# The opening of an attention and MLP kernel: q of the first unit turned by VectorE, filler products on TensorE, and other shapes of the first loads

## The chip, the cores and the metric

The kernel runs on one core of a Trainium2 chip. The metric is the device time of one execution in microseconds (us); lower is better. The median of three runs before the change is 677.4 us.

## The reference

Two blocks follow one another. The first is a gated linear attention with an outer-product state, over 4 batches x 8 heads, 768 tokens, head size 48:

```python
f = 1.0 / (1.0 + np.exp(-f_logit))
for t in range(S):
    state = f[:, :, t, :, None] * state + np.einsum('bhd,bhe->bhde', k[:, :, t], v[:, :, t])
    y[:, :, t] = np.einsum('bhd,bhde->bhe', q[:, :, t], state)
```

Its result, 3072 rows of 8 x 48 = 384 values, is the input x of the second block:

```python
h = x @ w_in                              # 384 -> 2048
g = h * (1.0 / (1.0 + np.exp(-1.702 * h)))
out = g @ w_out                           # 2048 -> 384
```

q, k, v, f_logit and the output are float32. The two weight matrices come in float64, and the kernel itself makes float32 of their bits.

## The kernel before, in words

The tokens are worked on in 12 units of 256 tokens, three to a batch, all heads of a unit at once. Feature and head lie on the partitions: two heads of a pair on partitions 0 to 47 and 64 to 111, and four pairs by 256 tokens along the free dimension (1,024 columns). The inputs come from memory with tokens on the partitions, so each of f, q and k of a unit has to be turned. Tile `raw` holds the three inputs as loaded (index j: 0 is f, 1 is q, 2 is k). `F` holds the turned gates after the sigmoid and `X` the turned k and q.

There are two ways to load and turn. For units below `N_FILL` = 3, `load_raw` (L243) loads by pair of heads, four transfers of 32 partitions each, and `turn` (L324) multiplies slices of `raw` by the identity on TensorE (L338) and lets ScalarE copy the result out of PSUM (L341). For later units `load_raw` loads two shifted copies of each head's rows (L257, `lo` = 0 and 32), and VectorE turns 32x32 blocks in one instruction (L326).

The attention of a unit goes through six levels (blocks of 1, 2, 4, ... 32 tokens). At each level TensorE makes scores of keys and queries (`score`, L383), VectorE multiplies keys and queries by the gates of the level (`promote`, L435 and L436 in the first three units, L438 later), masks the scores (`evacuate`, L409), and ScalarE sets keys aside (`set_aside`, L422). TensorE then multiplies the masked scores with v (L447). GpSimd makes the products of gates for all levels ahead of time (`begin_gates`, L375). In the first two units v is put in order by products with a permutation (`load_vl`, L283), copied out by ScalarE (L287). The result `yT` (L570) goes by transfer into `xT`, the input of the MLP.

The weights come in pairs of pieces (`fetch_weights`, L166, transfers at L179 into a tile `bits`). `begin_pair` has ScalarE scale the high words (L207, tile `a`), and a chain of five VectorE instructions for each piece (L222, L218, L225, L226, L227) makes float32 of them. `convert` sends one instruction of that chain, and the plan places these calls between the parts of attention.

The order of work on each engine is the order in which it is written; `merge` (L734) mixes parts of attention of unit n with MLP work of earlier units (L619 for the first product, L645 for the second) by shares of columns. All loads are issued by SyncE, in order. The opening (L769 to L784) issues the loads of unit 0 in the order f, q, k, then a first pair of weights, then v; turns f, q, k; sends four steps of conversion; fetches two more pairs of weights; and loads unit 1. Unit 0 has no MLP work to be mixed with.

```python
    for fn in units[0][0]:
        fn()
    for _ in range(4):
        convert()
```

`units[0][0]` is `(begin_f, begin, begin_k, begin_gates)`: turn f, turn q (with the edge copies on GpSimd at L356 and L357), turn k, products of gates.

Of the kernel before, what the change touches and what calls it, by code (L numbers as in the profile page):

```python
# [9 lines left out]
F32 = mybir.dt.float32  # L10
# [13 lines left out]
def kernel(  # L24
# [32 lines left out]
    nc = tc.nc  # L57
    B, H, S, D = q.shape
    DM = H * D
    DFF = moe_w_in.shape[1]  # L60
    P = 128
    C = 64
    G = 128
    U = 256
# [3 lines left out]
    NP = H // 2  # L68
# [7 lines left out]
    N_FILL = 3  # L76
# [10 lines left out]
    ps = ctx.enter_context(tc.tile_pool(name="ps", bufs=1, space=bass.MemoryType.PSUM))  # L87
# [9 lines left out]
    R = U // 32  # L97
    RW = R * D + HS - D
    raw = const.tile([P, 3, NP, R * D], F32, name="raw")
    by_pair = [raw.rearrange("p j a x -> p j (a x)")[:, j, :2 * RW].rearrange("p (h x) -> p h x", h=2) for j in range(3)]  # L100
    for j in range(3):
        nc.gpsimd.memset(by_pair[j][:, :, R * D:], 0.0)

    ident = const.tile([P, P], F32, name="ident")
# [2 lines left out]

    masks = const.tile([P, NL, 64], F32, name="masks")
    at = [wp.tile([P, 64], I32, tag="bits", name=f"at{j}", bufs=PAIRS_AHEAD) for j in range(2)]
    for a in (2, 3):  # L110
        nc.gpsimd.memset(raw[:, :, a, R * D - 32:], 0.0)
    nc.gpsimd.iota(at[0], pattern=[[0, 64]], base=0, channel_multiplier=1)
    nc.gpsimd.iota(at[1], pattern=[[1, 64]], base=0, channel_multiplier=0)
    nc.vector.tensor_scalar(at[0], at[0], 63, None, op0=ALU.bitwise_and)
# [125 lines left out]
            fetch_weights()  # L240


    def load_raw(n, j, engine=nc.sync):  # L243
        if n >= NALL:
            return
        b, s0 = n // NU, n % NU * U
        src = (f_logit, q, k)[j]
        if n < N_FILL:
            for a in range(NP):
                engine.dma_start(  # L250
                    out=by_pair[j][32 * a:32 * (a + 1), :, :R * D],
                    in_=src[b, 2 * a:2 * a + 2, s0:s0 + U, :].rearrange("h (i j) d -> i h (j d)", j=R),
                )
            return
        for r in range(4):
            lo = 32 * (r % 2)
            engine.dma_start(  # L257
                out=raw[32 * r:32 * (r + 1), j, :, :R * D - lo],
                in_=src[b, r // 2::2, s0:s0 + U, :].rearrange("a (i j) d -> i a (j d)", j=R)[:, :, lo:],
            )  # L260
# [30 lines left out]
    def load_vn(n):  # L291
        if n >= NALL:
            return
        vns[n] = (mlp if n == 1 else ld).tile([P, NG, DM], F32, tag="osb" if n == 1 else "vn", name=f"vn_{n}", bufs=1)
        if n < N_TURN:
            b, s0 = n // NU, n % NU * U
            for g in range(NG):
                nc.sync.dma_start(
                    out=vns[n][:, g].rearrange("p (h d) -> p h d", h=H),
                    in_=v[b, :, s0 + g * P:s0 + (g + 1) * P, :].rearrange("h p d -> p h d"),  # L300
                )
            return
        nc.sync.dma_start(out=vns[n], in_=v_toks[n % 2].rearrange("(g p) e -> p g e", g=NG))
# [8 lines left out]
    def attention(n):  # L312
# [9 lines left out]
            return lambda fn: parts.append((kind, fn))  # L322

        def turn(j, out, fn=None):  # L324
            if n >= N_FILL:
                nc.vector.transpose(  # L326
                    out.rearrange("p (a i j) -> p a j i", a=NP, j=R),
                    raw[:, j].rearrange("p a (j d) -> p (a j) d", j=R)[:, :, :32],
                )
                if fn:  # L330
                    nc.scalar.activation(out, out, fn)  # L331
                return
            for j0 in range(0, R, 4):
                pt = ps.tile([P, 4, P], F32, tag="mm", name=f"t_{n}_{j}_{j0}", bufs=4)
                for jj in range(4):
                    for h in range(2):
                        x = (j0 + jj) * D
                        nc.tensor.matmul(  # L338
                            pt[h * HS:(h + 1) * HS, jj, :], lhsT=by_pair[j][:, h, x:x + HS], rhs=ident, start=True, stop=True
                        )  # L340
                nc.scalar.activation(  # L341
                    out.rearrange("p (a i j) -> p a i j", a=NP, j=R)[:, :, :, j0:j0 + 4],
                    pt.rearrange("p j (a i) -> p a i j", a=NP), fn or AF.Copy,
                )

        def begin_f():
            turn(0, F, AF.Sigmoid)
            if n:
                load_raw(n + 1, 0)

        def begin():
            turn(1, X[:, J, 1:])


            q_last[n] = att.tile([P, NP], F32, tag="q_last", name=f"q_last_{n}", bufs=2)
            nc.gpsimd.tensor_copy(q_last[n], view(X, J * NX + U, [[U, NP]]))  # L356
            nc.gpsimd.tensor_copy(view(X, J * NX, [[U, NP]]), q_last[n - 1])  # L357
            if n:
                load_raw(n + 1, 1)

        def begin_k():
            turn(2, X[:, 1, :NA])
            if n:
                load_raw(n + 1, 2)
            if n >= N_FILL:
                set_aside(0, True)
                promote(0)
# [333 lines left out]
    units = [attention(n) for n in range(NALL)]  # L701
# [68 lines left out]
        load_raw(0, j)  # L770
    fetch_weights()
    load_vn(0)
    for fn in units[0][0]:
        fn()
    for _ in range(4):
        convert()
# [49 lines left out]
```

## Time and profile before

| | |
|---|---|
| three runs | 676.33, 677.4, 679.3 us |
| span of the profiled execution | 674.0 us |
| TensorE busy | 652.6 us (97%) |
| VectorE busy | 378.4 us (56%) |
| ScalarE busy | 226.4 us (34%) |
| first scores (L383) start | 12.46 us |
| first MLP product (L619) starts | 50.95 us |
| read from memory | 56.92 MB |

Engines: PE is TensorE, PEld its load of weights, DVE VectorE, ACT ScalarE, POOL GpSimd, SP SyncE, which issues the loads. A product in float32 leaves two MATMUL records. Times in the timeline count from the start of the span. In the slices each digit is the busy share of a 40th of the span in tenths. PEclk is the granted clock of TensorE. In the chain of waits each line is a start, a length and what the chain consisted of at that time. In the timeline, brackets give the idle time ahead of an instruction and what ended it. A transfer has an issue, which is what the SP rows show, and lands some time later.

### The profile page before, as it was taken

What the parts mean: (1) busy time and instruction counts of PE and PEld (TensorE: products, weight loads), DVE (VectorE), ACT (ScalarE), POOL (GpSimd) and SP (SyncE); (2) the same over time, 40 slices, a digit from 0 to 9 for tenths busy, and PEclk for the clock granted to TensorE, in tenths of its full rate; (3) what the DMA queues carried; (4) which work ended last, traced back from release to release, by engine and by line L of the source; (5) the groups of instructions that cost most, each with busy time, mean ns of one, the idle gap of its engine ahead of it and who ended that gap; (6) DMA issues with size and microseconds to landing.
All of it is one profiled execution on the core that took longest, in us unless ns stands there. A gap on an engine that the chain in (4) does not pass through costs nothing.

```text
span 674.0 us, 19354 instructions
## 1 busy us (share of the span) xinstructions
PE 652.6 (97%) x8514; PEld 486.5 (72%) x8514; DVE 378.4 (56%) x675; ACT 226.4 (34%) x459; POOL 50.3 (7%) x116
## 2 busy tenths in 40 slices
PE   5879999999999999999999999999999999999997
PEld 4656766757777886886886886876886786786774
DVE  3999877887666546545546546445446444430440
ACT  4564443343134233333333233233233233231210
POOL 3020020010002002002002002002002001000000
PEclk9789999999999999999999999999999999999999
DMA  8877973571063535415415415415414103001000
GB/s 193 226 192 193 240 160 89 152 185 37 24 159 107 154 66 149 109 38 148 115 33 152 110 37 148 113 37 144 115 37 115 37 24 84 15 1 36 13 1 24
DMA packets 67551, 67.62 MB, mean 100 GB/s; under 512 B 30410, under 2 KB 61290, under 8 KB 67466
## 3 DMA queue, kind: packets, MB, share of 16 engines
q1 hardware_dynamic: 67466, 66.38, 38.6%
q8 instruction: 67, 1.10, 0.7%
q14 instruction: 18, 0.15, 0.1%
HBM read 56.92 MB, written 8.65 MB: 97 GB/s over the span
## 4 chain that ended last, share of the span: by engine, by line
PE 89%; DVE 7%; ACT 2%; issue 1%; DMA 1%; SPq 0%; DVEq 0%; ACTq 0%
PE h L619 37%; PE o L645 35%; PE sc L383 5%; PE y L447 5%; PE t L338 2%; PE y L562 2%; PE tkn L504 1%; PE sc L522 1%; DVE s L218 1%; DVE A L409 1%; DMA xT<-yT 1%; PE tv L283 1%; ACT yT L570 1%; DVE X L436 1%; DVE X L438 1%
## 5 line engine op out<-in xcount | busy, mean ns | idle before, releaser
L619 PE MATMUL h<-xT,w_in 128*128 128x256 f32 (+1 forms) x1152 | 261.1, 382 | 1.1 <-DVE sum L690 0.8
L645 PE MATMUL o<-w_out,g 128*128 128x384 f32 x768 | 259.6, 491 | 0.9 <-DVE g L625 0.9
L619 PEld LDWEIGHTS h<-xT,w_in 128*128 128x128 f32 x1152 | 215.8, 190 | 36.8 <-issue 3.5
L645 PEld LDWEIGHTS o<-w_out,g 128*128 128x128 f32 x768 | 143.0, 190 | 94.5 <-issue 2.2
L625 DVE TENSOR_TENSOR g<-h,sg 128x256 f32<-128x256 f32 (+1 forms) x192 | 80.8, 422 | 133.1 <-ACT sg L624 132.6
L624 ACT ACTIVATE sg<-h 128x256 f32<-128x256 f32 (+1 forms) x192 | 73.2, 383 | 169.4 <-PE h L619 164.1
L422 ACT COPY Kc<-X 128x512 f32<-128x512 f32 x69 | 45.9, 666 | 123.7 <-DVE X L438 87.3
L438 DVE TENSOR_TENSOR X<-X,tot 128x1024 f32<-128x1024 f32 x45 | 55.2, 1226 | 54.8 <-PE sc L383 50.1
L409 DVE TENSOR_TENSOR A<-sc,masks 128x512 f32<-128x512 f32 x72 | 46.7, 679 | 0.0
L326 DVE STREAM_TRANSPOSE X<-raw 128x1024 f32<-128x1024 f32 x18 | 36.7, 2039 | 16.7 <-PE y L562 13.9
L447 PE MATMUL y<-A,vl 64*48 64x64 f32 x2304 | 41.7, 219 | 0.0
L447 PEld LDWEIGHTS y<-A,vl 64*48 64x48 f32 x2304 | 36.8, 122 | 5.3 <-issue 5.0
L375 POOL TENSOR_TENSOR tot<-F 128x512 f32<-128x512 f32 x12 | 12.5, 1039 | 340.5 <-DVE st L539 327.9
L383 PE MATMUL sc<-X,Kc 48*64 48x64 f32 x1344 | 29.0, 224 | 6.8 <-ACT Kc L422 4.6
L383 PEld LDWEIGHTS sc<-X,Kc 48*64 48x64 f32 x1344 | 24.6, 138 | 13.8 <-ACT Kc L422 7.2
L570 ACT COPY yT<-y 48x512 f32<-48x512 f32 x48 | 27.8, 580 | 20.0 <-PE y L562 19.4
L331 ACT ACTIVATE F<-F 128x1024 f32<-128x1024 f32 x9 | 9.5, 1057 | 49.0 <-DVE F L326 49.0
L375 POOL TENSOR_TENSOR tot<-tot 128x256 f32<-128x256 f32 (+4 forms) x60 | 23.7, 395 | 4.7
L542 DVE TENSOR_TENSOR st<-st,sc 128x192 f32<-128x192 f32 x44 | 15.6, 354 | 15.1 <-PE sc L522 13.7
L338 PE MATMUL t<-ident,raw 128*64 128x128 f32 x288 | 19.6, 298 | 4.4 <-DMA raw<-in_f_logit_dram 4.4
L338 PEld LDWEIGHTS t<-ident,raw 128*64 128x64 f32 x288 | 18.4, 153 | 7.0 <-issue 6.1
L664 ACT COPY osb<-o 128x384 f32<-128x384 f32 x18 | 8.6, 478 | 41.5 <-PE o L645 41.5
(66 smaller groups left out, 385.0 us busy)
## 6 DMA issues: line engine op xcount, KB each, us to landing
vl<-v_tok SPq DMA_DIRECT2D x60, 192.0 KB, 2.8
bits<-in_moe_w_out_dram SPq DMA_DIRECT2D x8, 768.0 KB, 9.8
bits<-in_moe_w_in_dram SPq DMA_DIRECT2D x8, 576.0 KB, 7.9
v_tok<-in_v_dram SPq DMA_DIRECT2D x10, 384.0 KB, 4.3
vn<-v_tok SPq DMA_DIRECT2D x10, 384.0 KB, 6.0
xT<-yT SPq DMA_DIRECT2D x24, 144.0 KB, 2.7
raw<-in_f_logit_dram SPq DMA_DIRECT2D x18, 192.0 KB, 3.9
raw<-in_q_dram SPq DMA_DIRECT2D x18, 192.0 KB, 3.1
```

Source lines behind the costliest of these rows:

```text
L326: nc.vector.transpose(out.rearrange("p (a i j) -> p a j i", a=NP, j=R), raw[:, j].rearrange("p a (j d) -> p (a j) d", j=R)[:, :, :32],)
L338: nc.tensor.matmul(pt[h * HS:(h + 1) * HS, jj, :], lhsT=by_pair[j][:, h, x:x + HS], rhs=ident, start=True, stop=True)
L375: nc.gpsimd.tensor_tensor(tn, t2[:, :, 0], t2[:, :, 1], ALU.mult)
L383: nc.tensor.matmul(out[g * HS:(g + 1) * HS, h, a, :], lhsT=lhs(h, a * U + g * G), rhs=rhs(h, a * U + g * G), start=True, stop=True,)
L409: nc.vector.tensor_tensor(A[:, :, c:c + w].rearrange("p h (x t) -> p h x t", t=64), t["sc"][:, :, c:c + w].rearrange("p h (x t) -> p h x t ...
L422: nc.scalar.copy(c.rearrange("p (n m) -> p n m", m=m), X[:, j, :NA].rearrange("p (n two m) -> p n two m", two=2, m=m)[:, :, hf, :],)
L438: nc.vector.tensor_tensor(qk, qk, by, ALU.mult)
L447: nc.tensor.matmul(dst(h, g, a), lhsT=vls[n, u][g * 64:(g + 1) * 64, (2 * a + h) * D:(2 * a + h + 1) * D], rhs=A(h, g, a), start=(start an ...
L619: nc.tensor.matmul(ph, lhsT=w_in[:, c, ff * P:(ff + 1) * P], rhs=xTs[n][:, c, :], start=(c == 0), stop=(c == NK - 1))
L624: nc.scalar.activation(sg, ph, AF.Sigmoid, scale=1.702)
L625: nc.vector.tensor_tensor(g[ff // FG][:, ff % FG, :], ph, sg, ALU.mult)
L645: nc.tensor.matmul(t["po"], lhsT=g[ff // FG][:, ff % FG, tt * P:(tt + 1) * P], rhs=w_out[:, ff, :], start=(ff == ffs[0]), stop=(ff == ffs[ ...
```

## The change

It concerns the start, before there is MLP work to fill TensorE. q of unit 0 is loaded in the form of the later units and turned by VectorE, which has nothing to do there. While TensorE waits for the first load, it makes six products of the identity with itself, into a tile that nothing reads; the intent is to have its clock raised when the real work comes. Units 0 to 2 load by head of a pair: two transfers of 128 partitions each instead of four of 32. k of unit 0 comes in two halves by token (four transfers), so that the first half can be turned while the second is under way. The order of the opening becomes f, gates, q, k. The memsets of the padding of `raw` are moved to fit: GpSimd now clears the tail of q's part in the later form for all four pairs.

```diff
-    for j in range(3):
+    for j in (0, 2):
         nc.gpsimd.memset(by_pair[j][:, :, R * D:], 0.0)
@@
-    for a in (2, 3):
-        nc.gpsimd.memset(raw[:, :, a, R * D - 32:], 0.0)
+    for a in range(NP):
+        nc.gpsimd.memset(raw[:, :, a, R * D - 32:] if a > 1 else raw[:, 1, a, R * D - 32:], 0.0)
@@
+    def by_vector(n, j):
+
+        return n >= N_FILL or (n == 0 and j == 1)
+
     def load_raw(n, j, engine=nc.sync):
...
-        if n < N_FILL:
-            for a in range(NP):
-                engine.dma_start(
-                    out=by_pair[j][32 * a:32 * (a + 1), :, :R * D],
-                    in_=src[b, 2 * a:2 * a + 2, s0:s0 + U, :].rearrange("h (i j) d -> i h (j d)", j=R),
-                )
+        if not by_vector(n, j):
+            for x in ((slice(0, R // 2), slice(R // 2, R)) if n == 0 and j == 2 else (slice(0, R),)):
+                for h in range(2):
+                    engine.dma_start(
+                        out=by_pair[j][:, h, x.start * D:x.stop * D],
+                        in_=src[b, h::2, s0:s0 + U, :].rearrange("a (i j) d -> a i (j d)", j=R)[:, :, x.start * D:x.stop * D],
+                    )
             return
@@
         def turn(j, out, fn=None):
-            if n >= N_FILL:
+            if by_vector(n, j):
                 nc.vector.transpose(
@@
-    for fn in units[0][0]:
+
+    warm = ps.tile([P, P], F32, tag="mm", name="warm", bufs=4)
+    for _ in range(6):
+        nc.tensor.matmul(warm, lhsT=ident, rhs=ident, start=True, stop=True)
+    begin_f, begin, begin_k, begin_gates = units[0][0]
+    for fn in (begin_f, begin_gates, begin, begin_k):
         fn()
```

On VectorE the change adds one instruction, the transpose, ahead of the first conversion (L222); the order behind it stays. On ScalarE it takes away the two copies of q. On SyncE there are ten issues ahead of the first weights instead of twelve.

## The prediction

> **What bounds the kernel now.** I read the page's slices first, to see where TensorE is not full.
>
> ```profile
> PE 652.6 (97%) x8514; PEld 486.5 (72%) x8514; DVE 378.4 (56%) x675; ACT 226.4 (34%) x459; POOL 50.3 (7%) x116
> ...
> PE   5879999999999999999999999999999999999997
> ...
> DVE  3999877887666546545546546445446444430440
> ...
> PEclk9789999999999999999999999999999999999999
> DMA  8877973571063535415415415415414103001000
> ```
>
> A slice is 16.85 us. From the fourth on TensorE is full, so what an opening saves is kept to the end. Only in the first three slices is something else the bound, and there VectorE shows a 9 from the second slice on. Next the chain of waits, asked for the first 75 us.
>
> ```profile
> 4.40 7.22 PE t L338 x96
> ...
> 11.70 0.46 ACT X L341
> 12.16 0.12 issue
> 12.28 0.99 ACT a L207 x2
> ...
> 13.61 1.16 DVE s L218 x2
> 14.77 0.62 DVE X L435
> ...
> 43.12 0.04 issue
> 43.16 0.48 PE y L562 x11
> ...
> 47.49 1.13 PE sc L383 x32
> ```
>
> The opening's turns (96 records at L338) lead to the last copy of X, ScalarE goes on to `a` (L207, the first weight pair), and from 13.3 to 43.1 the chain is VectorE almost without a break. That is 30 of the 47 us before TensorE takes over. The time is therefore set by the moment at which VectorE gets going. The timeline says what it waits for.
>
> ```profile
> 12.28 0.98 ACT L207 ACTIVATE a<-bits 128x384 f32<-128x384 f32 x2
> ...
> 12.85 0.83 DVE L222 TENSOR_SCALAR a<-a 128x384 int32<-128x384 int32 x2 [9.57 <-ACT a L207]
> ...
> 14.69 0.70 DVE L435 TENSOR_TENSOR X<-X,F 128x512 f32<-128x512 f32 x1
> ```
>
> VectorE sat idle for 9.57 us, and what released it was a conversion of weights, not the scores. The first product of attention with a gate (L435) stands behind four conversion instructions. So the load of the first weight pair (`bits`, from L179) matters as much as q, f and k. The completion records of the trace give its two transfers 11.52 and 12.12 us, the four of f 2.75 to 4.26, of q 4.79 to 6.14, of k 6.57 to 8.10, and v 13.08 and 14.19. In the kernel before ScalarE came free (12.28) just after the weights had landed (12.12): two ends within 0.2 us, of which the change moves one. Last, the issues and the loads by stage:
>
> ```profile
> 0.74 1.80 SPq L250 DMA_DIRECT2D raw<-in_f_logit_dram  x4
> 2.58 1.84 SPq L250 DMA_DIRECT2D raw<-in_q_dram  x4
> 4.46 1.84 SPq L250 DMA_DIRECT2D raw<-in_k_dram  x4
> 6.35 0.93 SPq L179 DMA_DIRECT2D bits<-in_moe_w_in_dram  x2
> ```
> ```profile
> 0.00:5.00 5.00, 0.60 (x6) 0.63 (x8) 1.25 (x8) 1.28 (x1) 2.40 (x20) 1.00 0.47 134
> 5.00:10.00 5.00, 5.00 (x68) 5.00 (x66) 0.00 (x0) 1.95 (x4) 0.00 (x0) 1.00 0.85 220
> 10.00:15.00 5.00, 3.91 (x66) 2.33 (x62) 2.06 (x5) 2.96 (x5) 3.65 (x8) 1.00 1.21 213
> ```
>
> The last two columns are the DMA share and GB/s. An issue takes 0.46 us and brings 98 kB, so the raw loads are paced by their issue, at about 210 GB/s. From 10 us on the engines are over-full.
>
> **What the Trainium skill says.** "TensorE: Matmul & The Clock Gate", What's actually happening: the array runs at half clock until a window of about 3.4 us has been busy, and windows run freely. The trace agrees: the first 40 records at L338 took 3.7 us (4.4 to 8.1), the next 41 took 1.8, and the low spells later (21.7 to 28.5, 45.6 to 52.4) last two windows each. The same page, Architectural detail: ScalarE and VectorE are strict FIFO; the 9.57 us above, with L435 behind it, agree. "DMA: Bandwidth & Descriptors", Queues, rings and completion order: loads issued on one queue share a ring per engine and are consumed in order. The landings above are in order of issue. So bytes put ahead of the weights delay the weights.
>
> **The change part by part.**
>
> *f.* Two transfers of 197 kB are issued by 1.6 us. First bytes came at 1.8 before; 393 kB at 210 to 300 GB/s end at 3.1 to 3.7 us, against 4.26.
>
> *Products of the identity.* Six full 128x128 products. The chain has 4 records of L504 (two products of this size) at 0.44 us with the clock up, so 0.44 each at half clock, and six last 2.6 us: about 1.5 (the identity is ready) to 4.1. They end when f is there; f itself gains 0.3 us at most from its earlier landing. They move the end of the half-clock spell from 8.0 towards 5 us. The 32 records of f then take 1.4 us (at full clock) to 3.0 (half); ScalarE's F is done at 6.3 to 7.8 against 8.7.
>
> *q by VectorE.* This removes 32 records at L338 and two ScalarE copies of 0.72 us, and adds one transpose of 2.04 us (the row of L326). It lies in VectorE's 9.57 us of idling, so it costs nothing if q is there by about 9.5. The price is bytes: q comes in the form with two shifted copies, 4 heads x 384 or 352 floats on 32 partitions, 753 kB in place of 393. A load of this form later in the trace (k, issued at 299.7) completed 5.0 us after its first issue. Here the first issue waits for a GpSimd memset (some 1.85 us against 1.6), so q lands near 6.9 and is turned near 8.9.
>
> *k in halves.* Four transfers of 98 kB, issued 3.6 to 5.4, land behind q at 7.3 to 8.6. Each half takes 16 records (0.7 us) and a ScalarE copy (0.72). The last X is done at 8.8 to 10.1 against 12.16.
>
> *First scores.* They start at about 9 to 10.3 us instead of 12.46. Behind them TensorE waits for v. The gates' products on GpSimd, now issued ahead of the edge of q, take 3.7 us from about 7 and are needed only after 15.
>
> *Weights.* All raw loads are now 1,533 kB against 1,180. At 225 to 290 GB/s from 1.8 us they end at 7.1 to 8.6; I take 7.7 (before: first weight packets at 7.4). The first weight pair then took 4.7 us, with a slow first microsecond (158 GB/s from 7 to 8 against 240 and 283 in the next two). As SyncE issues it 0.9 us sooner than before (10 transfers ahead in place of 12), part of that should be hidden: 3.8 to 4.7, I take 4.2. The pair lands at 10.9 to 13.3, by my values at 11.9. ScalarE, idle by then, starts `a` at 11.95 instead of 12.28. So of the 2 to 3.4 us that the scores gain, 0.3 us reach VectorE; the rest becomes a wait of ScalarE for `bits`, with `L222` and behind it `L435` waiting for that.
>
> *Later units.* Units 1 and 2 load with 6 transfers each in place of 12. SyncE waits less, but VectorE, full from 13 to 43 us, hides this. The second weight pair landed at 18.9 and was wanted by VectorE at 20.7 with 1 us of ScalarE between, so a gain above some 0.8 us would need that load to come sooner too.
>
> Sum: 677.4 - 0.3 = 677.1 us.
>
> **The rivals.** *The scores' gain arrives:* the weights land by about 9.5 and the chain starts where X is ready. For it: the DMA engines were only 70 to 72% busy from 3 to 7 us. Against it: 786 kB of weights behind 1,533 kB need 2,319 kB in 7.7 us, 300 GB/s, above any 5 us stretch shown. Partly so, gain 1.5 to 3 us: 675.0. *The doubled q delays the weights:* landing at 13.3, 1.0 us late, the second pair also late, and TensorE cold when its scores of unit 0 come, since it now idles from 10 to 13 us; plus 1.0 to 1.5: 678.7. For it: share 1.21 from 10 to 15; against it: the issue pacing that goes away. *Only the clock:* a half-clock spell at 45.6 to 52.4 falls into TensorE's own stretch from 47.5 on and costs about half of 4.9 us. Where the free windows fall decides whether it is one window or two: 1.7 us either way, in both kernels. It widens every case and favours none.
>
> **How the numbers follow.** Weights bound, 677.1: 0.63. Gain arrives, 675.0: 0.22. Weights later, 678.7: 0.15. With about 1.5 us of spread from the clock (before: 676.33 to 679.3) the range 674.5 to 679.3 leaves out about two in ten. Half a per cent is 3.4 us: faster than 674.0 needs the best of the first rival and a lucky clock, 0.10; slower than 680.8 the worst of the second, 0.05; within, 0.85.
>
> **What would show it.** Right: ScalarE's first `a` waits for the load of `bits`, near 12 us; VectorE's L222 follows within 0.8 us; the scores at L383 begin near 10 us and gain nothing. Wrong: if L222 starts before 11 us, the weights were not the bound and the time falls by about as much; if after 13, the second rival holds. The transpose of q ending after 12 us would show q's load mis-sized. If L222 starts on time and yet the end moves by more than 2 us, the reason lies after 43 us, most likely in the clock.

## The result and the profile after

The changed kernel takes 694.69 us (median of 4 runs, 694.1 to 695.11) against 677.46: a ratio of 1.0251, 95% interval 1.0227 to 1.0275. It is 17.2 us slower, far outside the stated range of 674.5 to 679.3.

The slices of the page after, in the same rows as before:

```profile
PE 660.1 (95%) x8494; PEld 491.4 (71%) x8494; DVE 380.2 (55%) x676; ACT 225.1 (32%) x457; POOL 49.3 (7%) x117
...
PE   5775998999999999999999999999999999999998
...
DVE  1795887778676645545545545545546444431450
...
PEclk9687999999999999999999999999999999999999
DMA  5675697267016443523523524514503202101000
```

The loss lies in the first four slices (17.3 us each). TensorE's fourth slice is a 5 where it was a 9, and VectorE's first is a 1 where it was a 3. The DMA row is lower there than before, 5675 against 8877, although more bytes are to be moved. The stretch up to TensorE's first MLP product, before (to 50.95 us) and after (to 67.70), says how large it is:

```profile
0.00:50.95 50.95, 36.73 (x840) 27.69 (x841) 37.92 (x88) 25.97 (x45) 10.06 (x36) 0.88 0.83 203
0.00:67.70 67.70, 42.62 (x821) 31.76 (x821) 40.56 (x92) 24.75 (x44) 8.83 (x37) 0.81 0.65 162
```

The columns are the stretch, its length, the busy time of TensorE, of its weight loads, of VectorE, ScalarE and GpSimd, then the granted clock, the DMA share and GB/s. Of the 19.0 us by which the two spans differ, 16.8 are there when the MLP starts. TensorE is idle for 10.9 us more and busy for 5.9 us more at a lower mean clock (0.81 against 0.88). So the core waits for loads, while its DMA engines are less busy than before. The chain of waits for the first 75 us of the kernel after:

```profile
1.55 8.00 DMA raw<-in_f_logit_dram
...
9.57 8.69 DMA raw<-in_k_dram
...
18.30 2.41 PE t L343 x18
...
35.98 9.46 DMA bits<-in_moe_w_out_dram
...
48.04 12.19 DMA bits<-in_moe_w_in_dram
60.23 7.43 DMA xT<-yT
```

Before, this chain held 2.15 us of loads. Now five transfers hold 46 us of it. The timeline after shows what this does to the instructions that the prediction named (line numbers are 5 to 10 higher here):

```profile
1.47 2.93 PE L781 MATMUL warm<-ident 128*128 128x128 f32 x12 [1.47 <-POOL ident masks.py:199]
...
9.60 3.67 PE L343 MATMUL t<-ident,raw 128*64 128x128 f32 x30 [2.70 <-DMA raw<-in_f_logit_dram]
...
12.82 2.02 DVE L331 STREAM_TRANSPOSE X<-raw 128x1024 f32<-128x1024 f32 x1 [9.47 <-DMA raw<-in_q_dram]
...
21.94 0.82 DVE L222 TENSOR_SCALAR a<-a 128x384 int32<-128x384 int32 x2 [7.10 <-ACT a L207]
```

The last field names the wait: f is complete at 9.6 us instead of 4.26, q is turned from 12.8, and VectorE's chain, which the prediction put at about 12.5, starts at 21.94. The six products missed their purpose here: they ended at 4.40, and the 30 records of f that begin at 9.60 took 3.67 us, where e1 below needs 2.78 for 32. By stage, for the kernel after (last two columns: DMA share and GB/s):

```profile
0.00:5.00 5.00, 2.93 (x12) 2.63 (x12) 1.26 (x8) 1.28 (x1) 2.47 (x21) 1.00 0.25 73
5.00:10.00 5.00, 1.08 (x6) 0.69 (x8) 0.00 (x0) 0.00 (x0) 0.00 (x0) 1.00 0.73 139
10.00:15.00 5.00, 4.00 (x34) 3.20 (x30) 2.02 (x1) 1.19 (x2) 1.01 (x1) 1.00 0.50 133
```

Before, the same stretches moved at 134, 220 and 213 GB/s. The completion records say why. In the kernel before, each transfer of f leaves 16 marks within 0.5 us (the first: 2.43 to 2.75). In the kernel after, each of the two transfers of f has one mark shortly after its issue (1.87 and 2.53 us) and four later: 5.44 to 6.17, and 9.15 to 9.56. Each transfer of q, which is cut in the other form, has twelve marks early and four late: 5.50 to 6.54, then 9.80 to 10.50 for the first of them. Read with one mark for each engine that ends its share, four of the sixteen engines carry f and k, the other twelve have no share of them, and four are late with their share of what is issued behind.

There is a second effect, on SyncE. It sends the third transfer of k at 6.19 us, directly behind the last mark of f's first transfer (6.17), and the fourth at 9.57, behind that of f's second (9.56). The first weights wait behind k and the last mark of q's first transfer (10.50):

```profile
4.17 6.34 SPq L255 DMA_DIRECT2D raw<-in_k_dram  x4
10.55 2.58 SPq L179 DMA_DIRECT2D bits<-in_moe_w_in_dram  x2
```

They were issued at 6.35 before. So the twelve engines, done with q at 9.08, have nothing to do until the weights go out. This is not the main part: in e3 below the weights go out at 6.22, and their last mark is still at 19.84, against 20.81 here.

The Trainium skill states the rule for the number of engines in "DMA: Bandwidth & Descriptors", Why a DMA increments its semaphore by 16 and not by 1: the number of engines is the largest one up to 16 that divides the size of the slowest dimension of both access patterns, they are the lowest-numbered ones, and the issuing engine makes up the missing marks at once. (Which of the sixteen they are, the marks here do not tell.) In the changed `load_raw` the memory side is `a (i j) d -> a i (j d)`, with the head of a pair outermost, 4 of them; before it was `i h (j d)`, with 32 token groups outermost. The marks, one early and four late, agree with four engines.

### The profile page after: what moved, and what is told of

It is laid out like the page before. It is cut to its first block, busy times and chain, and to the rows that moved or that the text cites. A ratio compares the mean times of both kernels' runs of the same rounds, so it can differ in the third digit from the quotient of the medians.

```text
span 693.0 us, 19290 instructions
## 1 busy us (share of the span) xinstructions
PE 660.1 (95%) x8494; PEld 491.4 (71%) x8494; DVE 380.2 (55%) x676; ACT 225.1 (32%) x457; POOL 49.3 (7%) x117
## 4 chain that ended last, share of the span: by engine, by line
PE 85%; DMA 7%; DVE 4%; ACT 2%; issue 1%; SPq 0%; DVEq 0%; ACTq 0%
PE h L624 36%; PE o L650 34%; PE sc L388 5%; PE y L452 4%; DMA xT<-yT 2%; DMA bits<-in_moe_w_in_dram 2%; PE y L567 1%; DMA bits<-in_moe_w_out_dram 1%; PE tkn L509 1%; PE sc L527 1%; DMA raw<-in_k_dram 1%; PE t L343 1%; DMA raw<-in_f_logit_dram 1%; DVE X L443 1%; DVE A L414 1%
## 5 line engine op out<-in xcount | busy, mean ns | idle before, releaser
L331 DVE STREAM_TRANSPOSE X<-raw 128x1024 f32<-128x1024 f32 x19 | 38.7, 2038 | 26.1 <-PE y L567 13.9
L380 POOL TENSOR_TENSOR tot<-F 128x512 f32<-128x512 f32 x12 | 12.5, 1039 | 348.9 <-DVE st L544 325.4
L343 PEld LDWEIGHTS t<-ident,raw 128*64 128x64 f32 x256 | 17.5, 157 | 11.8 <-DMA raw<-in_f_logit_dram 5.2
L547 DVE TENSOR_TENSOR st<-st,sc 128x192 f32<-128x192 f32 x44 | 15.6, 354 | 15.1 <-PE sc L527 13.7
```

What stands on the lines that cost most here:

```text
L331: nc.vector.transpose(out.rearrange("p (a i j) -> p a j i", a=NP, j=R), raw[:, j].rearrange("p a (j d) -> p (a j) d", j=R)[:, :, :32],)
L343: nc.tensor.matmul(pt[h * HS:(h + 1) * HS, jj, :], lhsT=by_pair[j][:, h, x:x + HS], rhs=ident, start=True, stop=True)
L380: nc.gpsimd.tensor_tensor(tn, t2[:, :, 0], t2[:, :, 1], ALU.mult)
```

## The experiments

Theory E: the outermost index of 4 puts the loads on four engines, and that is the whole loss. Rivals: transfers to 128 partitions, or fewer and larger ones, are slow in themselves; the doubled q delays the weights; TensorE's idle time and its clock make the loss.

**e1: all of the change, with the token group outermost.** The partitions are then in the order token group, head, so ScalarE reads the turned tile in that order.

```diff
-in_=src[b, h::2, s0:s0 + U, :].rearrange("a (i j) d -> a i (j d)", j=R)[...]
+in_=src[b, h::2, s0:s0 + U, :].rearrange("a (i j) d -> i a (j d)", j=R)[...]
-pt.rearrange("p j (a i) -> p a i j", a=NP)
+pt.rearrange("p j (i a) -> p a i j", a=NP)
```

> All of the change is kept, but in the transfers of f, k (and q of units 1 and 2) the index of the token group (32) stands ahead of the index of the head (4) in the memory pattern, so partitions are in the order token group, head; bytes, packets, count of transfers and the 128 partitions are those of the changed kernel. Theory E (four engines): a transfer whose outermost index counts 4 runs on 4 of the 16 DMA engines; with 32 outermost it runs on 16. Then f lands by 4 us instead of 9.6, the first scores start before 12 us, and the time is 675 to 679 us. Rival S (transfers to 128 partitions, or fewer transfers in flight, are slow): still 690 us or more. Rival Q (the 753 kB of q ahead of the weights are the delay): still 690 us or more.

Measured: 679.53 us, ratio to before 1.0006 (0.9993 to 1.0019). f is complete at 4.35, the first scores start at 11.71. Bytes, shapes and counts of transfers are those of the changed kernel, so rivals S and Q fall: the order of two indices (with the order in which ScalarE reads, which follows from it) is worth 2.4%. TensorE's busy time falls back with it, from 660.1 to 653.2 us (652.6 before), so the lower clock of the kernel after was a consequence of the waits. Against the kernel before, all of the change together then comes to nothing that is measured here. The later runs show that this is two effects of opposite sign.

**e2, e3, e4: the kernel before with nothing but the loads by head,** for units 0 to 2, for unit 0, and for units 1 and 2.

```diff
-for a in range(NP):
-    engine.dma_start(out=by_pair[j][32 * a:32 * (a + 1), :, :R * D],
-        in_=src[b, 2 * a:2 * a + 2, s0:s0 + U, :].rearrange("h (i j) d -> i h (j d)", j=R))
+for h in range(2):
+    engine.dma_start(out=by_pair[j][:, h, :R * D],
+        in_=src[b, h::2, s0:s0 + U, :].rearrange("a (i j) d -> a i (j d)", j=R))
```

> The kernel before, with nothing of the change but the loads by head of a pair for f, q and k of units 0 to 2 (two transfers of 128 partitions, head index of 4 outermost). Theory E: this alone makes the loss, 690 to 700 us; since q too is now on four engines in unit 0, rather more than the changed kernel. Rival Q (the doubled q) and a rival in which the idle TensorE and its clock make the loss: 676 to 680 us.

> The kernel before, with the loads by head for unit 0 alone. Theory E: the start of VectorE's chain moves by the later landing of k and the weights, as in the changed kernel (22.4 against 13.3 us): 9 to 13 us more, 686 to 690 us. If units 1 and 2 make most of the loss: under 680 us.

> The kernel before, with the loads by head for units 1 and 2 alone. Theory E: the waits for weights and for the first MLP input between 36 and 68 us (9.5, 12.2 and 7.4 us in the chain of the changed kernel), less what other work hides: 5 to 9 us more, 682 to 687 us; e3 and e4 together give about the loss of e2. If unit 0 makes the whole loss: under 679 us.

Measured: e2 694.96 us, ratio 1.0232 (1.0207 to 1.0257), the loss of the changed kernel without filler products and without VectorE's transpose. e3 684.57, ratio 1.0085 (1.0061 to 1.011). e4 687.22, ratio 1.0119 (1.0098 to 1.014). The parts, 5.8 and 8.1 us (0.0085 and 0.0119 of 678.99), make 13.9 of e2's 15.8. e4 came out at the upper edge of what I expected. e3 missed: VectorE's L222 moved by the expected 9.2 us (22.02 against 12.85) and TensorE's first MLP product by 8.8 (59.73 against 50.95), but the median by only 5.8. The two traces do not settle this. That of e3 is of its slowest execution (686.28 us, median 684.57), that of the kernel before is of one (675.73 us) faster than all 23 that ran beside e3 (677.25 to 681.65, median 678.99). This makes 5.0 of the 10.5 us between the two traced executions; where the slower executions of the kernel before lose their time is in no trace. In e4 the loads of unit 0 are those of before. From its chain of waits:

```profile
32.45 8.66 DMA bits<-in_moe_w_in_dram
...
52.94 7.45 DMA xT<-yT
```

The weights and the first MLP input, neither of which the change touched, wait for the four engines behind the loads of units 1 and 2. The marks show it: the first transfer of `xT`, issued at 50.94, has twelve marks from 53.10 to 53.62 and four from 58.91 to 59.80. TensorE's first MLP product (its line here is L626) shows what it costs:

```profile
60.48 4.24 PE L626 MATMUL h<-xT,w_in 128*128 128x256 f32 x10 [6.28 <-DMA xT<-yT]
```

It starts 9.5 us later than before (50.95), and 6.28 us of idling ahead of it end with `xT`.

**e11: two heads in each transfer,** unit 0 alone, everything else as before.

```diff
+for a in (0, 2):
+    for h in range(2):
+        engine.dma_start(out=by_pair[j][32 * a:32 * a + 64, h, :R * D],
+            in_=src[b, 2 * a + h:2 * a + h + 3:2, s0:s0 + U, :].rearrange("a (i j) d -> a i (j d)", j=R))
```

> As e3 (unit 0 by head, units 1 and 2 as before), but each transfer takes two of the four heads: 64 partitions, outermost index 2, twice as many transfers of half the size. Theory E: two engines carry f, q and k instead of four; in e3 1,180 kB took 15.6 us on four (19 GB/s each), so about 31 us here, k lands near 33 us and the time is 14 to 18 us over e3 (697 to 703 us). Rival (it is the shape of 128 partitions, or few large transfers, that is slow): no slower than e3, 676 to 686 us.

Measured: 698.73 us, ratio 1.0296 (1.0275 to 1.0318), 14.2 us over e3 by the medians. The transfers of f, q and k have two late marks each, and the last of k comes at 29.82 us (17.43 in e3, 8.10 before). By stage, for e11:

```profile
10.00:15.00 5.00, 3.62 (x32) 3.27 (x30) 0.00 (x0) 0.60 (x1) 0.00 (x0) 1.00 0.13 50
15.00:20.00 5.00, 1.04 (x8) 0.52 (x8) 0.00 (x0) 0.60 (x1) 0.00 (x0) 0.95 0.13 49
```

A DMA share of 0.13 is two sixteenths: two engines fully busy, at 25 GB/s each, and fourteen idle. Halving the outermost index halves the engines, with smaller transfers to fewer partitions. The rival of shape could not give this.

**e14: as e2, with the token group outermost** (the two lines of e1's diff are all that differs from e2).

> The kernel before with loads in two transfers of 128 partitions for units 0 to 2, as e2, but with the token group (32) outermost in the memory pattern instead of the head (4): e2 and this differ in the order of two indices and in the pattern with which ScalarE reads the turned tile. Theory E: about 677 us against 694.96 of e2, ratio to before 0.997 to 0.999 as in e12. Rival (two transfers of 128 partitions are bad whatever the order): over 690 us. If ratio is 1.000 or more, the gain of e12 came from k in halves or the changed order of the opening.

Measured: 676.91 us, ratio to before 0.9976 (0.9964 to 0.9987). Against e2's 694.96 this is the plainest pair: one order of two indices, with ScalarE's reading to match. The same stretches in e14:

```profile
0.00:5.00 5.00, 0.85 (x4) 0.48 (x6) 1.25 (x8) 1.28 (x1) 2.40 (x20) 1.00 0.51 149
5.00:10.00 5.00, 5.00 (x54) 5.00 (x54) 0.00 (x0) 1.30 (x3) 0.00 (x0) 1.00 0.98 244
```

It is also faster than the kernel before, by 0.24%. The cause of that gain is open. In the traces VectorE's L222 starts later than before (13.71 against 12.85) and yT is made no sooner (44.69 against 44.39), but the traced execution of the kernel before (675.73 us) is faster than all 25 beside e14 (from 675.9), and the traced one of e14 (677.62) is slower than its median, so these two traces cannot show a gain.

**What the rest of the change is worth** was tried on the repaired loads, because the prediction rested on it. e6 turns q of unit 0 on TensorE again (`by_vector` is `n >= N_FILL`, with the old memsets); e12 is e6 without the six products; e10 is the kernel before with the six products alone.

> As e1 (token group outermost, all else of the change), but q of unit 0 is loaded once (393 kB instead of 753) and turned by TensorE as before the change. My theory W (the first weights hold VectorE's chain, and the doubled q holds the weights): the weights land about 1 us sooner than in e1, VectorE's L222 starts at 12.6 to 13.0 us instead of 13.66, and the time is 0.5 to 1 us under e1 (ratio to before 0.998 to 0.9995). Rival (q's turn by VectorE is worth what the change wanted): slower than e1 by 1 us or more, since X is ready later.

> As e6 without the six products. If the loads in two transfers make e6's gain over before: 676.8 us, ratio 0.997 to 0.999, as e6. If the products (and where TensorE's clock then falls) make it: ratio 0.9995 to 1.001. X is ready at 12 us or later, close to the landing of the weights at 12.5.

> The kernel before with the six products of the identity alone. Theory W (the first weights hold VectorE's chain): the turns end about 1.5 us sooner (96 records in 5.7 us as in e6 instead of 7.2), X is ready near 10.6 us, and ScalarE then waits for the weights, which land at 12.1 as before; L222 at 12.7 against 12.85, ratio 0.9985 to 1.0005. Rival (the turns hold the chain): L222 near 11.3 us and 1.5 us less (ratio 0.998 or lower).

Measured: e6 676.76, ratio 0.998 (0.9971 to 0.999); e12 677.32, ratio 0.9975 (0.9963 to 0.9987); e10 677.83, ratio 0.9988 (0.9976 to 0.9999). In e6 L222 starts at 13.14, sooner than e1's 13.66 though later than I had said. The first weights land at 12.48 there against 13.00 in e1, so q's second copy (360 kB and two more issues) delays them by 0.5 us. In time it costs more: between e1 (1.0006) and e6 (0.998) lie 0.26%, 1.8 us, and TensorE's first MLP product starts at 52.95 in e1 and at 51.18 in e6. How 0.5 us becomes 1.8, and which part the turn on VectorE has, no run separates. e10's ratio lies inside what theory W allowed, but its interval also holds the 0.998 of its rival; its trace decides:

```profile
12.10 0.71 PE L383 MATMUL sc<-X 48*64 48x64 f32 x32 [0.86 <-ACT X L341]
12.49 0.99 ACT L207 ACTIVATE a<-bits 128x384 f32<-128x384 f32 x2 [0.44 <-DMA bits<-in_moe_w_in_dram]
13.08 0.81 DVE L222 TENSOR_SCALAR a<-a 128x384 int32<-128x384 int32 x2 [9.80 <-ACT a L207]
```

The products shorten the turns (96 records in 6.52 us against 7.21), but ScalarE is then ready and waits for `bits`, and L222 is not sooner than before (12.85). e12, without products, keeps the gain of e6, and e14, with neither k in halves nor the new order of the opening, has it too, so it comes with the loads in two transfers.

**Taking the weights out of the way.** e7 is e1, and e13 is e6, with the four conversions behind unit 0's parts; e8 is the kernel before with the first weights fetched ahead of f, q and k and six conversions ahead of the turns.

```diff
-    for _ in range(4):
-        convert()
     fetch_weights()
...
     merge(0, fill, 0, steady, 8)
+    for _ in range(4):
+        convert()
```

> As e1, but the four first conversion instructions of VectorE stand behind the parts of unit 0 instead of ahead of its first gate product. Theory W: the first gate product (L440 here) no longer waits for weights; it starts at about 12.6 us instead of 15.3, and of these 2.7 us the part in which VectorE was idle is kept, some 1 us; the conversions themselves are only moved. Time 0.5 to 1.2 us under e1. Rival (the scores, not the weights, hold the chain): L440 does not start sooner than 14.5 us and the time is that of e1.

> As e6 with the first four conversion instructions behind the parts of unit 0. From e7 (2.3 us earlier gate product, no gain in time) I expect no more than 0.5 us over e6: ratio 0.997 to 0.999. If without the doubled q the earlier start is kept: 0.9955 to 0.997.

> The kernel before, with the first pair of weights fetched ahead of f, q and k and six conversion instructions ahead of the turns. Theory W: the weights land at about 5 us, VectorE converts in the time in which it idled (L222 near 6 us against 12.85), f, q and k land about 2 us later (k near 10.3), but TensorE's turns were longer than the loads and X is ready at 12.5 to 13.5 us against 12.41; the first gate product starts at 13.5 to 14.5 instead of 14.77 with two conversions more behind it. Time 1 to 2.5 us under before (ratio 0.996 to 0.9985). Rival (the opening's start is held by f, q, k and the turns alone): slower than before by about 2 us.

Measured: e7 679.22, ratio 1.001 (0.9998 to 1.0022); e13 680.06, ratio 1.0017 (1.0007 to 1.0028); e8 679.04, ratio 1.0011 (0.9999 to 1.0022). All three missed their ranges. e7 does what it should at the start, and gives it back. The timeline of e7:

```profile
13.05 0.69 DVE L440 TENSOR_TENSOR X<-X,F 128x512 f32<-128x512 f32 x1 [1.93 <-PE sc L388]
...
17.16 1.01 ACT L207 ACTIVATE a<-bits 128x384 f32<-128x384 f32 x2
17.75 0.81 DVE L222 TENSOR_SCALAR a<-a 128x384 int32<-128x384 int32 x2 [2.81 <-ACT a L207]
...
19.41 0.69 DVE L440 TENSOR_TENSOR X<-X,tot 128x512 f32<-128x512 f32 x1
```

The first gate product is at 13.05 instead of 15.31, but ScalarE now scales the weights behind its work for the first level, VectorE idles 2.81 us for it, and the second gate product comes at 19.41 against 18.59 in e1. In e8 the weights land at 6.54, ScalarE then first loads a table for 1.28 us, and L222 starts at 8.48, but f is there only at 8.1 us, TensorE's turns end near 15.7, and VectorE idles 6.62 us before its first gate product at 17.39. VectorE's chain has two suppliers, and in e7 and e8 bringing one forward let the other or a later one bind. e13 starts as e7 does (first gate product 12.48, second 20.32).

## Why the prediction was wrong

**The step that failed** is the first: "393 kB at 210 to 300 GB/s end at 3.1 to 3.7 us". It gave the new transfers the rate of the old ones. They ran on four engines, so f came at 9.56 us, k at 18.26 (said: 7.3 to 8.6) and the first weights at 20.81 (said: 10.9 to 13.3). The cause, shown by e1, e11 and e14, stood in the diff, and the page of the skill that I cited for the order of queues states the rule in another section. I looked at the partitions that a transfer writes, 128, and not at the outermost index that it reads, 4.

**"Units 1 and 2 load with 6 transfers each in place of 12. SyncE waits less"**: counted as nothing. Alone (e4) it costs 8.1 us, against 5.8 for unit 0 alone (e3); I looked at the number of issues and not at where the bytes would queue. Work that the change did not touch (weights, `xT`) paid, since its shares on the four engines lay behind.

**The signs of being wrong.** L222 after 13 us was to mean that the second rival holds, the doubled q. It started at 21.94, but e2 has no doubled q and loses about as much (1.0232). The transpose of q ended at 14.84, after the 12 us that were to show its load mis-sized. That sign was right, but the missing engines were the reason and not the bytes.

**The second rival** named a delay of the weights by the doubled q and put 1.0 to 1.5 us on it. It has no part in the 17, but on 16 engines the runs speak for it: L222 starts at 13.66 in e1, after the 13 that was its sign, and e1 lies 1.8 us over e6.

**What held, and what was luck, once the loads run on 16 engines (e1).** The time was put at 677.1 against 677.4, a gain of 0.3; measured 1.0006 (0.9993 to 1.0019), in which such a gain fits. This is luck: the loads in two transfers gain about 0.2% (e6, e12, e14), which the prediction did not have, and the doubled q with its turn on VectorE costs about as much, which its main case took to be made up by a sooner issue of the weights. The wait came as stated, ScalarE's first `a` waiting for `bits`:

```profile
11.71 0.71 PE L388 MATMUL sc<-X 48*64 48x64 f32 x32 [0.86 <-ACT X L346]
13.08 0.98 ACT L207 ACTIVATE a<-bits 128x384 f32<-128x384 f32 x2 [1.43 <-DMA bits<-in_moe_w_in_dram]
13.66 0.80 DVE L222 TENSOR_SCALAR a<-a 128x384 int32<-128x384 int32 x2 [3.19 <-ACT a L207]
```

The weights landed at 13.0 where I took 11.9 of a stated 10.9 to 13.3. One term that was wrong here is "SyncE issues it 0.9 us sooner". I had taken 0.46 us for an issue from the transfers of 32 partitions. In e1 the two of f, to 128 partitions, took 1.31 us, the four of k 2.48, and the weights went out at 6.68, 0.3 us later than before (6.35). f came at 4.35, not at 3.1 to 3.7, and had gained nothing. The scores come at 11.71, not at 9 to 10.3: q landed at 8.27 (said: 6.9), its transpose ended at 10.46 (8.9), k came at 9.50 (to 8.6). The products took 2.93 us against 2.6 and nearly filled the wait for f, which was turned from 4.34. The transpose took 2.07 us in e1, close to the 2.04 of its row, within VectorE's idle time.

Two smaller slips change nothing above: the raw loads add up to 1,540 kB and not 1,533, and the load at 299.7 from which q was sized completed after 5.2 us and not 5.0.

**"The time is therefore set by the moment at which VectorE gets going"** holds in one direction only. A later start costs time (e3, 5.8 us). A first gate product 2.3 us sooner (e7) gave nothing: the conversions had only been moved, and VectorE met other waits behind its first link.

## What to carry to other kernels

Read a transfer's pattern for the size of its outermost index on both sides, in memory and on chip, before taking a rate for it: with 4 there it ran on four of the sixteen engines, and the two orders of the same two indices lay 18 us apart. The loss does not stay with that transfer: loads that came behind on all sixteen engines had their last four marks up to 7 us after the other twelve (weights issued at 45.81 in the kernel after: 52.45, then 59.28), and what needed them waited for those. In the profile the signs are a low DMA share beside waits for loads, and completion marks that come in two groups. A second sign is the queue that issues the loads: while it waits for a slow transfer, the idle engines get no work either.

## What the runs showed that I had not expected

- Two engines alone moved 50 GB/s at a DMA share of 0.13 (e11), 25 GB/s for each. On four, f, q and k of e3 were complete at 17.43 us: 1,180 kB in about 15.6 us, 19 GB/s for each. That average has a slow beginning in it: the first of the six transfers ended at 5.63, the other five, 983 kB, in the next 11.8 us, 21 GB/s for each.
- On 16 engines the transfers of twice the size and half the number are good: e14, e6 and e12 are 0.2 to 0.25% faster than the kernel before, each with an interval below 1, and no trace shows where. Why stays open.
